# Sigmoid attention with a SiLU layer behind it: w_in's second half in two steps, and another order at the end

## Chip, cores and metric

The kernel runs on one core of one Trainium2 chip. The metric is the device time of one execution in microseconds (us); times of several runs are given by their median. TensorE is called PE, VectorE DVE, ScalarE ACT, GpSimd POOL and SyncE SP, as in the profile.

## What is computed

Eight batches of 448 tokens, with 12 heads of 64 each, go through attention with a sigmoid in place of the softmax; the result, 3584 tokens by 768, goes through a layer of 2048 hidden units with SiLU.

```python
scores = scale * np.matmul(q, k.transpose(0, 1, 3, 2)) - np.log(S)   # q, k, v: (8, 12, 448, 64)
attn = 1.0 / (1.0 + np.exp(-scores))
attn_out = np.matmul(attn, v)
x = attn_out.transpose(0, 2, 1, 3).reshape(B * S, H * D)             # (3584, 768)
h = x @ w_in                                                         # w_in: (768, 2048)
g = h * (1.0 / (1.0 + np.exp(-h)))
out = g @ w_out                                                      # w_out: (2048, 768)
```

All inputs and the output are float32 in DRAM. The kernel multiplies in float16.

## The kernel before

**Tiles.** The heads are taken four at a time, two pairs of them, as a *quad*; a batch has three quads, and there are 24 in all, numbered 0 to 23. A quad's k, q and v lie in the tiles kf, qf and vf, 224 KB each. k and q are transposed to kT and qT: for quads 0 to 5 by matmuls against an identity (pe_transpose, L143), for later ones by DMA transposes. The scores of a quad come in seven tiles (scores, L174), whose sigmoid ACT writes to attnT (L181); values (L205) multiplies them with v into xT, the transposed input of the layer.

**The layer.** For the first two batches, h_unit (L240) makes the hidden units in 16 chunks of 128 columns of w_in (fc 0 to 15), six matmuls each. Chunks 0 to 3 read w_in's first quarter of columns, 4 to 7 the second, 8 to 11 the third, 12 to 15 the fourth. From chunk 8 of the first batch on, w_in_sums also lets DVE form sums of w_in's halves (L280 to L284). Later batches are taken two at a time with a Strassen-Winograd scheme on such sums (h_pair, L316). The output product works in the same way: out_set takes two blocks of 128 tokens, a1 and a2, and seven products of eight matmuls (product, L463), each followed by one or two additions on DVE (plus, L473) that gather the four parts c11, c12 (tile osb[0], block one) and c21, c22 (osb[1], block two), each 128 x 384.

**Order.** The order on each engine is that of the program text. On PE the chunks of the layer are a generator that is advanced between the attention's bursts by their cost in ns; after the last burst the rest of it runs straight through. So the last call of out_set, with last=True, is the end of the kernel, and only DVE's additions and the stores stand behind its last product.

**Loads.** All loads but that of the first q are issued by POOL on one DMA queue, in program order, and cast to float16 on the way. load(names, g) issues one DMA per name. load_w_in(step, steps) issues two DMAs, each for half of w_in's rows: 384 KB each for a quarter of the columns, 768 KB each for half of them. after_transpose and after_values fix the order. It is, from w_in on: w_in quarter 0; k and q of quad 4; w_in quarter 1; k and q of quad 5; v of quad 3; w_in quarters 2 and 3 in one step; v of quad 4; w_out's parts 0 and 2; v of quad 5; k and q of quad 6; w_out part 1; k and q of quad 7; w_out part 3. The transposes of k and q of quads 4 and 5 stand between bursts 0, 1, 2 and 4 of the first stretch in which layer and attention are mixed.

**Stores.** store writes an osb tile to the output, 64 token rows with each of two DMAs, on the queues that it is given: whole rows (192 KB a DMA) or columns left or right (96 KB a DMA). In the last call the left half of block one is stored by SP alone after c11; block two is stored whole, one half of its rows by SP and the other by ACT, after c21; and c12 is made in two pieces of 192 columns, each with eight matmuls of its own, an addition, and a store of 48 KB by SP and one by ACT.

Of the kernel before, what the change touches and what calls it, by code (L numbers as in the profile page):

```python
# [17 lines left out]
def kernel(  # L18
# [9 lines left out]
    nc = tc.nc  # L28

    B, H, S, D = q.shape  # L30
    NT, DMODEL = out.shape
    DFF = moe_w_in.shape[1]
# [8 lines left out]
    NO2 = DMODEL // 2  # L41
    NQB = NQ * B
    NHC = NFC // 2
# [22 lines left out]
    def new_flat(name, g):  # L66
        flat[name, g] = (p3 if name == "v" else p4).tile(
            [P, 2, NCH, D], F16, tag=f"{name}f", name=f"{name}f"
        )

    def rows_in(name, g):
        b, iq = divmod(g, NQ)
        return (
            source[name][b]
            .rearrange("(j h) s d -> j h s d", j=2)[:, 2 * iq : 2 * iq + 2]
            .rearrange("j h (p c) d -> (h p) j (c d)", c=NCH)
        )

    def load(names, g, c0=0, c1=NCH):
        for name in names:  # L80
            if (name, g) not in flat:
                new_flat(name, g)
            nc.gpsimd.dma_start(  # L83
                flat[name, g][:, :, c0:c1].rearrange("p j c d -> p j (c d)"),
                rows_in(name, g)[:, :, c0 * D : c1 * D],
            )
# [13 lines left out]
    w_in_of = w_in_sb.rearrange("p (q h) f -> p h q f", h=2)  # L100
    w_out_sb = cpool.tile([P, NFC, DMODEL], F16, tag="w_out_sb", name="w_out_sb")

    def load_w_in(step, steps=1):
        cols = slice(step * DFF // 4, (step + steps) * DFF // 4)
        for j in range(2):
            rows = slice(j * DMODEL // 2, (j + 1) * DMODEL // 2)
            nc.gpsimd.dma_start(
                w_in_sb[j * D : (j + 1) * D, :, cols],
                moe_w_in[rows, cols].rearrange("(cc d) f -> d cc f", d=D),
            )  # L110

    def load_w_out(part):
        fcs = slice(part * NFC // 4, (part + 1) * NFC // 4)
        nc.gpsimd.dma_start(
            w_out_sb[:, fcs],
            moe_w_out[part * DFF // 4 : (part + 1) * DFF // 4].rearrange("(fc p) e -> p fc e", p=P),
        )
# [182 lines left out]
    def h_pair(m, tail):  # L300
# [112 lines left out]
    wq = [  # L413
        [w_out_sb[:, r * NHC : (r + 1) * NHC, c * NO2 : (c + 1) * NO2] for c in range(2)]
        for r in range(2)
    ]
    tw = {}
# [18 lines left out]
    def block(g):  # L436
        return gTr[:, :, g * P : (g + 1) * P]

    def row_blocks(m, g):
        return [rows_of[2 * m + u // NCH, u % NCH] for u in (2 * g, 2 * g + 1)]  # L440

    def out_set(a1, rows1, a2, rows2, scale, tail=(), last=False, halves=False):
        nonlocal hold
        lo, hi = slice(0, NHC), slice(NHC, NFC)
        osb = [p3.tile([P, DMODEL], F32, tag="osb", name="osb") for _ in range(2)]
        c11, c12 = (osb[0][:, nh * NO2 : (nh + 1) * NO2] for nh in range(2))
        c21, c22 = (osb[1][:, nh * NO2 : (nh + 1) * NO2] for nh in range(2))
        m1 = p3.tile([P, S], F32, tag="m1", name="m1")[:, :NO2]
        between, *sg = tail or [None]
        for i in range(len(sg) + 1, 4):  # L450
            sg.append(cpool.tile([P, NHC, P], F16, tag=f"S{i}", name=f"S{i}"))

        def store(rows, o, cols, engines):
            for at, (row, eng) in enumerate(zip(rows, engines)):
                eng.dma_start(row[:, cols], o[at * HP : (at + 1) * HP, cols])

        left, right, whole = slice(0, NO2), slice(NO2, DMODEL), slice(0, DMODEL)

        def product(a, w, between=None):
            po = ps_1.tile([P, 512], F32, tag="ps1", name="po")  # L460
            n = w.shape[2]
            for fc in range(NHC):
                nc.tensor.matmul(  # L463
                    po[:, :n], a[:, fc, :], w[:, fc, :], start=(fc == 0), stop=(fc == NHC - 1)
                )
                if fc < NHC - 1:
                    yield 163
                if between and fc == NHC // 2 - 1:
                    yield from between()
            return po[:, :n]  # L470

        def plus(o, po, x, sign=1.0):
            nc.vector.scalar_tensor_tensor(  # L473
                out=o, in0=po, scalar=sign * scale, in1=x, op0=ALU.mult, op1=ALU.add
            )

        if not tail:
            nc.vector.tensor_sub(sg[2], a1[:, lo], a2[:, lo])
            nc.vector.tensor_add(sg[0], a2[:, lo], a2[:, hi])
        po = yield from product(a1[:, lo], wq[0][0], between)  # L480
        nc.scalar.activation(m1, po, AF.Copy, scale=scale)
        sg.append(cpool.tile([P, NHC, P], F16, tag="S4", name="S4"))
        if not tail:
            nc.vector.tensor_sub(sg[1], sg[0], a1[:, lo])
        hold = False
        yield 163
        if tail:
            po = yield from product(sg[2], tw[3])
            plus(c22, po, m1)
            yield 163  # L490
        po = yield from product(a1[:, hi], wq[1][0])
        plus(c11, po, m1)
        nc.vector.tensor_sub(sg[3], a1[:, hi], sg[1])
        if last or halves:
            store(rows1, osb[0], left, (nc.sync, nc.sync))
        yield 163
        if not tail:
            po = yield from product(sg[2], tw[3])
            plus(c22, po, m1)
            yield 163  # L500
        po = yield from product(sg[1], tw[2])
        both = c21 if last else c22
        plus(both, po, c22)
        plus(c12, po, m1)
        yield 163

        def minus():
            po = yield from product(a2[:, hi], tw[4])
            plus(c21, po, both, -1.0)
            if not last:  # L510
                yield 163

        if not last:
            yield from minus()
        po = yield from product(sg[0], tw[1])
        plus(c22, po, both)
        plus(c12, po, c12)
        if last:
            yield 163
            yield from minus()  # L520
        store(rows2, osb[1], whole, (nc.sync, nc.scalar if last else nc.sync))
        yield 163
        for c0 in (0, NO2 // 2) if last else (0,):
            c1 = NO2 // 2 + c0 if last else NO2
            po = yield from product(sg[3], wq[1][1][:, :, c0:c1])
            plus(c12[:, c0:c1], po, c12[:, c0:c1])
            if last:
                store(rows1, osb[0], slice(NO2 + c0, NO2 + c1), (nc.sync, nc.scalar))
        if not last:
            store(rows1, osb[0], right if halves else whole, (nc.sync, nc.sync))  # L530
        yield 163

# [23 lines left out]
            if b * NFC + fc in rows_at:  # L556
                rows_of_quad(*rows_at[b * NFC + fc], act_copy)

    HALVES = 0

    def moe_set(m, g, tail=()):
        scale = ISX if m == 0 else 1.0
        step = out_set(
            block(g),
            row_blocks(m, g),
            block(g + 1),
            row_blocks(m, g + 1),
            scale,
            tail,
            halves=(m == B // 2 - 1 and g >= HALVES),  # L570
        )
        for i, ns in enumerate(step):
            if m % 2 == 0 and g == 2 and i % 8 == 4 and i < 32:
                fcs = slice(i // 8 * 4, i // 8 * 4 + 4)
                nc.vector.tensor_scalar_mul(kept[:, fcs], block(NCH - 1)[:, fcs], scale)
            if m == 0 and g == 2 and i in (36, 44, 52):
                next(in_sums)
            if m == 0 and g == 0 and i in (2, 8, 14, 20):
                next(sums)
            yield ns  # L580
# [59 lines left out]
    def after_transpose(g):  # L640
        if g == 0:
            load_w_in(0)
            load("kq", 4)
            load_w_in(1)
        elif g == 1:
            load("kq", 5)

    def after_values(g):
        if g == 0:
            load("v", 3)  # L650
            load_w_in(2, 2)
        elif g == 1:
            load("v", 4)
            load_w_out(0)
            load_w_out(2)
        elif g == 2:
            load("v", 5)
            load("kq", 6)
            load_w_out(1)
            load("kq", 7)  # L660
            load_w_out(3)
        elif 4 < g < NQB - 3:
            load("v", g + 3)
# [29 lines left out]
    def transposes(g, name):  # L693
        pe_transpose(g, ((name, 0, 4), (name, 4, NCH)))
        if name == "q":
            after_transpose(g)
# [82 lines left out]
    n = 2 * NT_B  # L779
    for m in range(1, B // 2):  # L780
        stop = min(2 * (m + 1) * NT_B + 4, len(units))
        bursts = bursts_to(n, stop)
        n = stop
# [51 lines left out]
```

## Time and profile before

| | us |
|---|---|
| median of 3 runs | 364.54 |
| the three runs | 363.94, 364.54, 367.28 |
| the profiled execution, its own time | 367.21 |
| its span, first to last instruction | 365.1 |
| busy in the span: ACT | 249.7 |
| busy in the span: DVE | 265.0 |

The profile is of one execution. Its times count from the start of its span. In a timeline row the columns are start, duration, engine, line, operation, tile written and tiles read with shapes, and the number of instructions merged in the row; the bracket gives the engine's idle time before and what ended it. In a windows row there follow, after the bounds, the busy time and count of PE, PE's weight loads, DVE, ACT and POOL, then the granted PE clock as a share of the full one, the share of the DMA engines and GB/s. In a DMA row the columns are what is written and read, the issuing queue, the operation, count, size of one and the time from issue to landing.

### The profile page before, as it was taken

Reading aid. Unit: us, or ns where it says so; the run is one execution under the profiler, and the core shown is the slowest. Engines: PE = TensorE matmul, PEld = TensorE weight load, DVE = VectorE, ACT = ScalarE, POOL = GpSimd, SP = SyncE. Lnnn points to the kernel's source line nnn. Section 1 sums busy time; section 2 is a strip of 40 time slices with the busy share of each in tenths; the row PEclk is TensorE's granted clock in tenths of the full one; section 3 lists DMA queues with packets and bytes.
Section 4 is the critical chain, followed back from the end, with each engine's and each line's share of the span. In section 5 each row is a group of like instructions: output and inputs, shape, how many; then the busy total and the mean of one; then the engine's idle time right before and its main releaser. Section 6 shows DMA issues by size and latency. Waiting matters only on the chain.

```text
span 365.1 us, 7677 instructions
## 1 busy us (share of the span) xinstructions
PE 355.9 (97%) x3029; PEld 182.9 (50%) x3029; DVE 265.0 (73%) x498; ACT 249.7 (68%) x363; POOL 61.8 (17%) x103
## 2 busy tenths in 40 slices
PE   8999799999999999999999999999999999999995
PEld 4544345444454555555445455555445455556663
DVE  3647479887879678787677667786777677778773
ACT  5998587697778767678777767758888766660000
POOL 8543210412505001100222201200100000000000
PEclk9999899999999999999999999999999999999999
DMA  8999999999899838405999752731965020003333
GB/s 136 196 205 210 208 206 170 135 195 139 139 202 175 147 95 114 59 0 96 172 165 216 148 113 50 105 49 24 154 95 133 19 69 0 3 0 87 88 87 85
DMA packets 63106, 42.78 MB, mean 117 GB/s; under 512 B 36064, under 2 KB 59232, under 8 KB 63072
## 3 DMA queue, kind: packets, MB, share of 16 engines
q0 software_dynamic: 24096, 22.58, 41.3%
q1 hardware_dynamic: 38592, 19.21, 26.9%
q10 hardware_dynamic: 384, 0.52, 0.4%
q8 instruction: 23, 0.38, 0.4%
q14 instruction: 11, 0.09, 0.1%
HBM read 45.61 MB, written 11.01 MB: 155 GB/s over the span
## 4 chain that ended last, share of the span: by engine, by line
PE 89%; DMA 9%; DVE 1%; issue 0%
PE po L463 36%; PE hy L316 11%; PE psc L174 10%; PE ph L240 8%; PE hz L316 7%; PE hx L316 7%; PE pav L205 7%; DMA w_in_sb<-in_moe_w_in_dram 5%; DMA kf<-in_k_dram 3%; DMA qs<-in_q_dram 1%; DVE qT L150 1%; PE ptrq L143 0%; PE pw L130 0%; PE ptrk L143 0%; DVE qf L633 0%
## 5 line engine op out<-in xcount | busy, mean ns | idle before, releaser
L181 ACT ACTIVATE attnT<-psc 128x896 f16<-128x896 f32 x168 | 144.9, 922 | 32.5 <-PE psc L174 29.9
L463 PEld LDWEIGHTS <-S 128*128 128x128 f16 x456 | 42.2, 98 | 35.5 <-issue 10.4
L174 PE MATMUL psc<-qT,kT 64*64 64x448 f16 x672 | 52.2, 361 | 1.0 <-DVE qT L150 0.7
L473 DVE SCALAR_TENSOR_TENSOR osb<-po,osb 128x384 f32<-128x384 f32 (+1 forms) x71 | 37.8, 549 | 15.9 <-PE po L463 15.0
L221 DVE TENSOR_SCALAR xT<-pav 128x448 f16<-128x448 f32 x44 | 25.6, 620 | 26.0 <-PE pav L205 26.0
L327 ACT ACTIVATE gTr<-u 128x448 f16<-128x448 f32 x48 | 27.6, 575 | 23.2 <-DVE u L340 19.1
L240 PE MATMUL ph<-xT,w_in_sb 128*128 128x448 f16 x192 | 40.5, 361 | 2.7 <-DMA w_in_sb<-in_moe_w_in_dram 2.6
L463 PE MATMUL po<-w_out_sb,S 128*128 128x384 f16 (+1 forms) x232 | 41.5, 321 | 0.0
L463 PE MATMUL po<-T,S 128*128 128x384 f16 x224 | 41.3, 327 | 0.0
L316 PEld LDWEIGHTS <-w_in_sb 128*128 128x128 f16 x288 | 28.2, 98 | 26.1
L463 PEld LDWEIGHTS <-gTr 128*128 128x128 f16 x304 | 28.3, 98 | 23.2 <-issue 5.8
L205 PE MATMUL pav<-attnT,vf 64*64 64x448 f16 x672 | 37.5, 349 | 0.0
L463 PE MATMUL po<-w_out_sb,gTr 128*128 128x384 f16 x192 | 35.7, 327 | 0.0
L316 PE MATMUL hy<-xs,w_in_sb 128*128 128x448 f16 x144 | 35.1, 353 | 0.0
L316 PE MATMUL hx<-xT,w_in_sb 128*128 128x448 f16 x144 | 34.6, 353 | 0.0
L316 PEld LDWEIGHTS <-W 128*128 128x128 f16 x216 | 21.1, 98 | 19.6
L174 PEld LDWEIGHTS <-kT 64*64 64x64 f16 x672 | 16.2, 104 | 28.8 <-issue 24.2
L83 POOL DMA_DIRECT2D vf<-in_v_dram x24 | 17.2, 718 | 71.6 <-PE psc L174 70.0
L240 PEld LDWEIGHTS <-w_in_sb 128*128 128x128 f16 x192 | 17.7, 99 | 23.0 <-issue 8.9
L473 DVE SCALAR_TENSOR_TENSOR osb<-po,m 128x384 f32<-128x384 f32 x42 | 23.0, 553 | 6.4 <-PE psc L174 1.7
L253 DVE TENSOR_TENSOR gTr<-ph,tsig 128x448 f16<-128x448 f32 x32 | 19.8, 623 | 9.1 <-ACT tsig L252 8.9
L205 PEld LDWEIGHTS <-vf 64*64 64x64 f16 x672 | 20.1, 107 | 11.5 <-issue 1.1
(76 smaller groups left out, 414.4 us busy)
## 6 DMA issues: line engine op xcount, KB each, us to landing
out_dram<-osb SPq DMA_DIRECT2D x47, 192.0 KB, 3.2
vf<-in_v_dram POOLq DMA_DIRECT2D x24, 224.0 KB, 7.8
kf<-in_k_dram POOLq DMA_DIRECT2D x23, 224.0 KB, 5.8
qf<-in_q_dram POOLq DMA_DIRECT2D x23, 224.0 KB, 6.8
w_out_sb<-in_moe_w_out_dram POOLq DMA_DIRECT2D x4, 768.0 KB, 18.4
w_in_sb<-in_moe_w_in_dram POOLq DMA_DIRECT2D x4, 384.0 KB, 11.4
w_in_sb<-in_moe_w_in_dram POOLq DMA_DIRECT2D x2, 768.0 KB, 15.1
out_dram<-osb SPq DMA_DIRECT2D x14, 96.0 KB, 2.2
```

What stands on the lines that cost most here:

```text
L83: nc.gpsimd.dma_start(flat[name, g][:, :, c0:c1].rearrange("p j c d -> p j (c d)"), rows_in(name, g)[:, :, c0 * D : c1 * D],)
L150: (copy[0] if copy else nc.vector.tensor_copy)(dst[:, c0 * P : c1 * P], ptr[:, : (c1 - c0) * P])
L174: nc.tensor.matmul(psc[own, j, :S], qkT["k", g][rows, ch, own], qkT["q", g][rows, :, own], start=True, stop=True,)
L181: nc.scalar.activation(attnT[g, ch], psc[:, :, :S], AF.Sigmoid, bias=NEG_LOG_S, scale=QKSCALE)
L205: nc.tensor.matmul(pav[half][j * D : (j + 1) * D, :S], flat["v", g][own, j, ch, :], at[own, j, :], start=(ch == 0), stop=(ch == NCH - 1),)
L221: nc.vector.tensor_scalar_mul(xT[b][:, half * NQ + iq, :], pav[half][:, :S], SX)
L240: nc.tensor.matmul(ph[:, :S], w_in_of[:, cc // NQ, cc % NQ, fc * P : (fc + 1) * P], xT[b][:, cc, :], start=(at == 0), stop=(at == NCC - 1),)
L253: nc.vector.tensor_mul(gTr[:, fc, (b % 2) * S : (b % 2) * S + S], ph[:, :S], tsig)
L316: nc.tensor.matmul(ps, a[:, c, i * P : (i + 1) * P], bs(c), start=(first and c == 0), stop=(c == HCC - 1), skip_group_check=True,)
L327: nc.scalar.activation(gTr[:, side * NHC + i, odd * S : (odd + 1) * S], src, AF.Silu, scale=ISX)
L463: nc.tensor.matmul(po[:, :n], a[:, fc, :], w[:, fc, :], start=(fc == 0), stop=(fc == NHC - 1))
L473: nc.vector.scalar_tensor_tensor(out=o, in0=po, scalar=sign * scale, in1=x, op0=ALU.mult, op1=ALU.add)
```

## The change

Three things are changed.

w_in's second half is loaded in two steps of a quarter each, so by four DMAs of 384 KB instead of two of 768 KB. The place in the queue is the same.

q of quad 4 is issued behind w_in's second quarter instead of ahead of it.

In the last call of out_set, the product that is subtracted (a2[hi] with tw[4], for c21) moves from behind the product of sg[0] with tw[1] to ahead of it, as in all other calls. Block two is stored in two halves of its columns, the left behind c21 and the right behind c22, each with one DMA of 96 KB on SP and one on ACT. The last product, of sg[3] with wq[1][1], is made with eight matmuls of 384 columns, one addition, and one store of 96 KB on each of the two queues. The variable HALVES, which was 0 and so changed nothing, goes.

```diff
-    def load_w_in(step, steps=1):
-        cols = slice(step * DFF // 4, (step + steps) * DFF // 4)
+    def load_w_in(step):
+        cols = slice(step * DFF // 4, (step + 1) * DFF // 4)
...
         po = yield from product(sg[1], tw[2])
-        both = c21 if last else c22
-        plus(both, po, c22)
+        plus(c22, po, c22)
         plus(c12, po, m1)
         yield 163
-
-        def minus():
-            po = yield from product(a2[:, hi], tw[4])
-            plus(c21, po, both, -1.0)
-            if not last:
-                yield 163
-
-        if not last:
-            yield from minus()
+        po = yield from product(a2[:, hi], tw[4])
+        plus(c21, po, c22, -1.0)
+        if last:
+            store(rows2, osb[1], left, (nc.sync, nc.scalar))
+        yield 163
         po = yield from product(sg[0], tw[1])
-        plus(c22, po, both)
+        plus(c22, po, c22)
         plus(c12, po, c12)
         if last:
-            yield 163
-            yield from minus()
-        store(rows2, osb[1], whole, (nc.sync, nc.scalar if last else nc.sync))
+            store(rows2, osb[1], right, (nc.sync, nc.scalar))
+        else:
+            store(rows2, osb[1], whole, (nc.sync, nc.sync))
         yield 163
-        for c0 in (0, NO2 // 2) if last else (0,):
-            c1 = NO2 // 2 + c0 if last else NO2
-            po = yield from product(sg[3], wq[1][1][:, :, c0:c1])
-            plus(c12[:, c0:c1], po, c12[:, c0:c1])
-            if last:
-                store(rows1, osb[0], slice(NO2 + c0, NO2 + c1), (nc.sync, nc.scalar))
-        if not last:
+        po = yield from product(sg[3], wq[1][1])
+        plus(c12, po, c12)
+        if last:
+            store(rows1, osb[0], right, (nc.sync, nc.scalar))
+        else:
             store(rows1, osb[0], right if halves else whole, (nc.sync, nc.sync))
         yield 163
...
         if g == 0:
             load_w_in(0)
-            load("kq", 4)
+            load("k", 4)
             load_w_in(1)
+            load("q", 4)
...
             load("v", 3)
-            load_w_in(2, 2)
+            load_w_in(2)
+            load_w_in(3)
```

More of the change, by code (lines that the diff above doesn't have):

```diff
@@ L460, in product @@
             po = ps_1.tile([P, 512], F32, tag="ps1", name="po")
-            n = w.shape[2]
             for fc in range(NHC):
                 nc.tensor.matmul(
-                    po[:, :n], a[:, fc, :], w[:, fc, :], start=(fc == 0), stop=(fc == NHC - 1)
+                    po[:, :NO2], a[:, fc, :], w[:, fc, :], start=(fc == 0), stop=(fc == NHC - 1)
                 )
@@ L469, in product @@
                     yield from between()
-            return po[:, :n]
+            return po[:, :NO2]
         def plus(o, po, x, sign=1.0):
@@ L557, in moe_h @@
                 rows_of_quad(*rows_at[b * NFC + fc], act_copy)
-    HALVES = 0
     def moe_set(m, g, tail=()):
@@ L569, in moe_set @@
             tail,
-            halves=(m == B // 2 - 1 and g >= HALVES),
+            halves=(m == B // 2 - 1),
         )
```

## Prediction

> **What bounds the kernel now.** I read the page first: busy time, the granted clock by slices, the chain of waits.
>
> ```profile
> span 365.1 us, 7677 instructions
> PE 355.9 (97%) x3029; PEld 182.9 (50%) x3029; DVE 265.0 (73%) x498; ACT 249.7 (68%) x363; POOL 61.8 (17%) x103
> ...
> PEclk9999899999999999999999999999999999999999
> ...
> PE 89%; DMA 9%; DVE 1%; issue 0%
> ```
>
> TensorE (PE) is busy for 97% of the span and carries 89% of the chain, so time is won only where PE stands still or runs slowly, or behind its last product. The one dent in the granted clock is the fifth slice, 36.5 to 45.6 us. The chain in order of time and the waits of PE name the place.
>
> ```profile
> 24.83 16.55 DMA w_in_sb<-in_moe_w_in_dram
> 41.52 0.92 PE ph L240 x4
> ...
> 324.87 35.78 PE po L463 x228
> ```
>
> ```profile
> PE ph L240 <- DMA w_in_sb<-in_moe_w_in_dram: 2.6, 1, 2.6
> ```
>
> The chain hangs on a w_in load issued at 24.83 and landing 16.55 later, at 41.38; from 41.52 it is nearly all PE. The timeline of PE there, and the windows that hold the clock (column after the five engines), show the price.
>
> ```profile
> 31.03 0.58 PE L143 MATMUL ptrq<-ident,qf 128*64 128x128 f16 x14
> 34.36 1.88 PE L240 MATMUL ph<-xT,w_in_sb 128*128 128x448 f16 x9
> 38.19 0.74 PE L240 MATMUL ph<-xT,w_in_sb 128*128 128x448 f16 x3
> 41.52 0.92 PE L240 MATMUL ph<-xT,w_in_sb 128*128 128x448 f16 x4 [2.59 <-DMA w_in_sb<-in_moe_w_in_dram]
> 42.87 0.96 PE L143 MATMUL ptrq<-ident,qf 128*64 128x128 f16 x14
> 43.76 3.07 PE L240 MATMUL ph<-xT,w_in_sb 128*128 128x448 f16 x9
> ```
>
> ```profile
> 43.00:43.50 0.50, 0.50 (x12) 0.50 (x13) 0.00 (x0) 0.50 (x1) 0.06 (x1) 0.50 1.17 212
> 46.50:47.00 0.50, 0.50 (x10) 0.14 (x8) 0.03 (x1) 0.32 (x1) 0.05 (x1) 1.00 1.24 208
> ```
>
> PE stands still for 2.59 us before the first product on w_in's second half (chunk fc 8). Then the clock is at 0.50: the 14 transposes take 0.96 instead of 0.58, the 9 products 3.07 instead of 1.88. Stall and slow clock cost 2.59 + 0.38 + 1.19 = 4.16 us.
>
> The Trainium skill, "TensorE: Matmul & The Clock Gate", Part 1, says that the clock is judged over a free-running window of 3413 ns and halved after an idle one, and its closing table warns of gaps over about 3 us. The trace agrees on the half clock, but shows it behind a gap of only 2.59 us. By the free phase the same gap would be punished in some executions and not in others.
>
> **Part 1, w_in's second half in two steps.** The timeline of GpSimd (POOL) has the issues of v of quad three, of the later of the two big loads, of w_in's second quarter (two) and of v of quad five; the DMA view behind it gives the time from issue to landing (last column) of these five in the same order.
>
> ```profile
> 21.74 0.70 POOL L83 DMA_DIRECT2D vf<-in_v_dram  x1 [0.80 <-PE psc L174]
> 24.83 0.66 POOL L107 DMA_DIRECT2D w_in_sb<-in_moe_w_in_dram  x1 [0.85 <-DMA kf<-in_k_dram]
> 16.09 0.66 POOL L107 DMA_DIRECT2D w_in_sb<-in_moe_w_in_dram  x1 [1.16 <-DMA vf<-in_v_dram]
> 17.22 0.66 POOL L107 DMA_DIRECT2D w_in_sb<-in_moe_w_in_dram  x1 [0.47 <-DMA kf<-in_k_dram]
> 30.75 0.70 POOL L83 DMA_DIRECT2D vf<-in_v_dram  x1 [0.40 <-issue]
> ```
>
> ```profile
> vf<-in_v_dram POOLq DMA_DIRECT2D x1, 224.0 KB, 11.4
> w_in_sb<-in_moe_w_in_dram POOLq DMA_DIRECT2D x1, 768.0 KB, 16.5
> w_in_sb<-in_moe_w_in_dram POOLq DMA_DIRECT2D x1, 384.0 KB, 11.5
> w_in_sb<-in_moe_w_in_dram POOLq DMA_DIRECT2D x1, 384.0 KB, 12.1
> vf<-in_v_dram POOLq DMA_DIRECT2D x1, 224.0 KB, 19.7
> ```
>
> v of quad three lands at 21.74 + 11.4 = 33.14 and the last big load at 41.38, so the 2 x 768 KB take 8.24 us. Cut into four loads of 384 KB at the same rate, 2.06 each, w_in's third quarter is there at 33.14 + 4.12 = 37.26. The small loads of the second quarter land at 27.59 and 29.32, 1.73 apart; by that it is 36.6. PE wants it at 38.19 + 0.74 = 38.93. I take 37.26: the stall goes with 1.67 us to spare, and the slow clock with it, since no gap is left in front of it.
>
> The fourth quarter still lands at about 41.4. Its first product is the 25th from 41.52 on:
>
> ```profile
> 51.09 1.31 PE L240 MATMUL ph<-xT,w_in_sb 128*128 128x448 f16 x6
> 55.63 1.52 PE L205 MATMUL pav<-attnT,vf 64*64 64x448 f16 x28
> ```
>
> It falls in the first of these rows, at 51.09 - 4.16 = 46.9 or later, 5.5 us behind its load. The four 0.66-us issues lie on POOL, busy for 17%. The bytes ahead of every later load are unchanged, so later landings stay where they are while their readers come up to 4.16 us earlier. The nearest is v of quad five: it lands at 30.75 + 19.7 = 50.45, read from 55.63 - 4.16 = 51.47. That is 1.0 us of cover.
>
> **Part 2, quad four's q behind the second quarter.** It moves back past two loads of 384 KB and lands where the second of them did, at 29.32. Its transposes start at 31.03: 1.7 us of cover, cost nothing. Each microsecond beyond that would be one of PE. The second quarter gains one q load of time, which PE does not need.
>
> **Part 3, the end.** The rows are of the timeline, then of the DMA view. The product order changes (the subtracted product before the c22 one), with the same matmuls; the 16 narrow matmuls become 8 wide ones.
>
> ```profile
> 357.86 1.46 PE L463 MATMUL po<-T,gTr 128*128 128x384 f16 x8
> 359.16 1.48 PE L463 MATMUL po<-w_out_sb,S 128*128 128x192 f16 x16
> 357.24 0.55 DVE L473 SCALAR_TENSOR_TENSOR osb<-po,m 128x384 f32<-128x384 f32 x1
> 360.68 0.36 DVE L473 SCALAR_TENSOR_TENSOR osb<-po,osb 128x192 f32<-128x192 f32 x1 [0.30 <-PE po L463]
> 361.15 0.83 SPq L455 DMA_DIRECT2D out_dram<-osb  x1
> 361.50 0.72 ACTq L455 DMA_DIRECT2D out_dram<-osb  x1
> ```
>
> ```profile
> out_dram<-osb ACTq DMA_DIRECT2D x1, 48.0 KB, 2.6
> out_dram<-osb SPq DMA_DIRECT2D x14, 96.0 KB, 2.2
> out_dram<-osb ACTq DMA_DIRECT2D x1, 192.0 KB, 3.4
> ```
>
> Eight wide matmuls take 1.46 where 16 narrow ones take 1.48: PE ends 0.02 earlier. The last addition is 0.55 instead of 0.36: 0.19 later, from 360.66 to 361.21. SP issues 0.11 after it now (361.04 to 361.15), but ACT only at 361.50, behind its own earlier stores. With the block before stored in halves, its left half leaves once the subtracted product is added, near 358.7, so both queues should be free and issue at 361.32. The last landing is now 361.50 + 2.6 = 364.1. For the new 96 KB stores the bounds are 2.2 (a store alone) and 3.4 (192 KB beside another queue); I take 2.6, nearest to a last store with both queues in use: 363.92. The end gains 0.2, bounds +0.6 and -0.6.
>
> **The sum** on the profiled execution, 367.21 (span 365.1 and 2.1 around it), is 367.21 - 4.16 - 0.2 = 362.85. Of the three runs, two lie at 363.94 and 364.54 and one at 367.28, as long as the profiled one. So the median, 364.54, lacks 2.67 us that the profile shows. If all of it sits in stall and clock, the changed median is 362.85; if only the 1.57 us of slow clock does, it is 364.54 - 2.59 - 0.2 = 361.75. Nothing shown parts these two, and I take the middle: **362.3 us**, on its own 361.4 to 363.5 with the end's bounds.
>
> **The rivals.**
> First, the median run carries the whole 4.16 and the 2.67 comes from elsewhere: 364.54 - 4.16 - 0.2 = 360.2. For it: stall and clock are the only large losses that PE shows. Against it: a difference of 3 us between runs fits a gap that is punished in some and not in others.
>
> Second, the loads don't do what they say: the third quarter still lands after 38.93 because four loads on one queue share its rate and finish together, or the median has no stall at all. Then only the end is left: 364.3. Against it: landings in the trace come in order of issue, 1.73 us apart for the small ones.
>
> Third, slower: every load has a fixed cost, and two more of them push the whole queue back. Price: a 96 KB store takes 2.2 us alone, nearly all of it fixed. Two more loads would then put v of quad five at 50.45 + 4.4 = 54.85, read at 51.47: PE stands still for 3.4 us in a new place and pays the slow clock again, 362.3 + 3.4 + 1.57 = 367.3. It decides from 1.0 us of delay on, and makes the kernel slower than its median from about 1.7. Against it: 2 x 384 KB need 3.5 us in the queue by the 1.73 above, less than the 4.12 of one 768 KB load, so the fixed part seems to lie beside other transfers.
>
> The Trainium skill speaks for this rival: "DMA: Bandwidth & Descriptors", Rules for kernel authors, asks for 1 MiB or more per DMA, and its section on the anatomy of one DMA fits about 2.0 us plus the bytes. By that 2.0 the third rival would give an estimated 366.9; the 1.73 us between landings goes against adding it per load.
>
> **How the numbers follow.** Forecast 0.50, first rival 0.24, second 0.13, third 0.13. The range takes in the first two rivals with the end's bounds: 359.8 (360.2 less 0.4) to 365.0 (364.3 and up to 0.7); the third stays out. A measurement of this kernel can tell about 1% from no change, 3.6 us. Below 360.9: the first rival and 0.03 of the forecast, 0.27. Above 368.2: the worse part of the third rival, 0.05. Between: 0.68.
>
> **What would show it.** Part 1: the first product on the second half waits for nothing, w_in's third quarter lands near 37.3, the clock has no 0.50 rows near 43, and PE's wait for w_in is gone from the list. Part 2: no wait of the transposes at 31 for q. Part 3: last addition 0.55, last stores issued together near 0.1 behind it. Wrong would be a new wait of PE for v of quad five or for q, PE idle of more than 0.5 us between 36 and 52, or a changed median under 360.9 or over 363.5.

## The result and the profile after

| | before | changed |
|---|---|---|
| median of 21 runs, us | 364.31 | 363.35 |
| lowest and highest, us | 363.05, 370.08 | 361.94, 364.60 |
| ratio of the times, 95% interval | | 0.9965 [0.9949, 0.9981] |
| profiled execution, its span, us | 367.21, 365.1 | 361.94, 360.1 |

The change is worth 0.35% by the ratio (0.2 to 0.5%), which is 1.3 us, and 1.0 us by the medians. The two profiled executions differ by 5.3 us, so they are not typical ones; the first is one of the long executions of the kernel before, the second the shortest of the changed kernel. Six of the 21 executions of the kernel before took more than 366 us, and two of 80 in the later sets; why they are long was not followed up. What an ordinary one looks like came out of further profiles, below.

The page of the changed kernel first: span, PE's busy time, the granted clock and the chain.

```profile
span 360.1 us, 7663 instructions
PE 354.0 (98%) x3021; PEld 181.7 (50%) x3021; DVE 264.6 (73%) x497; ACT 249.6 (69%) x363; POOL 63.0 (17%) x105
...
PEclk9999999999999999999999999999999999999999
...
PE 94%; ACT 3%; DMA 1%; DVE 1%; issue 0%
```

The dent in the clock is gone, and no w_in load is left in the chain. The timeline of PE at w_in's second half, and all the waits of PE in this execution:

```profile
38.05 1.50 PE L240 MATMUL ph<-xT,w_in_sb 128*128 128x448 f16 x7
39.48 0.57 PE L174 MATMUL psc<-qT,kT 64*64 64x448 f16 x8
```

```profile
PE pw L130 <- DVE warm L620: 1.1, 1, 1.1
PE psc L174 <- DVE qT L150: 0.7, 2, 0.4
```

The last three matmuls of chunk 7 and the first four of chunk 8 run as one row of seven: nothing separates them. The issues of the last load of w_in's third quarter and of the last of its fourth, and behind them their times to landing:

```profile
23.69 0.66 POOL L107 DMA_DIRECT2D w_in_sb<-in_moe_w_in_dram  x1 [0.50 <-DMA kf<-in_k_dram]
27.70 0.66 POOL L107 DMA_DIRECT2D w_in_sb<-in_moe_w_in_dram  x1 [1.46 <-DMA w_in_sb<-in_moe_w_in_dram]
```

```profile
w_in_sb<-in_moe_w_in_dram POOLq DMA_DIRECT2D x1, 384.0 KB, 11.9
w_in_sb<-in_moe_w_in_dram POOLq DMA_DIRECT2D x1, 384.0 KB, 11.7
```

They land at 35.6 and 39.4. The end, in the timeline and the DMA view:

```profile
354.70 1.46 PE L462 MATMUL po<-w_out_sb,S 128*128 128x384 f16 x8
356.20 0.56 DVE L472 SCALAR_TENSOR_TENSOR osb<-po,osb 128x384 f32<-128x384 f32 x1 [0.28 <-PE po L462]
356.79 0.47 SPq L455 DMA_DIRECT2D out_dram<-osb  x1
356.79 0.50 ACTq L455 DMA_DIRECT2D out_dram<-osb  x1
```

```profile
out_dram<-osb SPq DMA_DIRECT2D x1, 96.0 KB, 2.1
out_dram<-osb ACTq DMA_DIRECT2D x1, 96.0 KB, 2.4
```

Both last stores go out at once, 0.03 us behind the addition. From the start of the last product to the end of the span it is 360.1 - 354.70 = 5.40 us, where it was 365.1 - 359.16 = 5.94. This stretch hardly depends on what came before it: in the six profiles with the old end it is 5.93 to 6.02, in the six with the changed end 5.39 to 5.48. So one profile gives it to about 0.1.

### The profile page after: what moved, and what is told of

Its sections match the earlier page's. It is cut to its first block, busy times and chain, and to the rows that moved or that the text cites. A ratio compares the mean times of both kernels' runs of the same rounds, so it can differ in the third digit from the quotient of the medians.

```text
span 360.1 us, 7663 instructions
## 1 busy us (share of the span) xinstructions
PE 354.0 (98%) x3021; PEld 181.7 (50%) x3021; DVE 264.6 (73%) x497; ACT 249.6 (69%) x363; POOL 63.0 (17%) x105
## 4 chain that ended last, share of the span: by engine, by line
PE 94%; ACT 3%; DMA 1%; DVE 1%; issue 0%
PE po L462 37%; PE hy L316 11%; PE psc L174 11%; PE ph L240 11%; PE pav L205 8%; PE hz L316 8%; PE hx L316 8%; ACT attnT L181 3%; DMA qs<-in_q_dram 1%; PE ptrk L143 1%; PE ptrq L143 1%; DVE qT L150 1%; PE pw L130 0%; DVE qf L623 0%; DVE osb L472 0%
## 5 line engine op out<-in xcount | busy, mean ns | idle before, releaser
L472 DVE SCALAR_TENSOR_TENSOR osb<-po,osb 128x384 f32<-128x384 f32 x70 | 37.6, 554 | 15.8 <-PE po L462 15.0
L462 PE MATMUL po<-w_out_sb,S 128*128 128x384 f16 x224 | 41.3, 327 | 0.0
L240 PE MATMUL ph<-xT,w_in_sb 128*128 128x448 f16 x192 | 39.2, 353 | 0.0
L383 DVE TENSOR_TENSOR u<-hy,p 128x448 f32<-128x448 f32 x24 | 15.0, 625 | 13.8 <-PE hy L316 13.4
```

Of the source, the lines that this page charges most:

```text
L240: nc.tensor.matmul(ph[:, :S], w_in_of[:, cc // NQ, cc % NQ, fc * P : (fc + 1) * P], xT[b][:, cc, :], start=(at == 0), stop=(at == NCC - 1),)
L383: nc.vector.tensor_add(u3, y, p1)
L462: nc.tensor.matmul(po[:, :NO2], a[:, fc, :], w[:, fc, :], start=(fc == 0), stop=(fc == NHC - 1))
L472: nc.vector.scalar_tensor_tensor(out=o, in0=po, scalar=sign * scale, in1=x, op0=ALU.mult, op1=ALU.add)
```

## The experiments

The ratio is to the kernel before, timed beside it on the same chip; it is not the quotient of two medians. The kernels were timed in three sets: the first four of the table (the kernel before at 364.34 there), the next three (364.32), and the last two, on another chip (364.03). Medians are compared within a set.

| kernel | median, us | ratio, 95% interval |
|---|---|---|
| new loads alone (e1_loads) | 364.16 | 0.9985 [0.9963, 1.0006] |
| new end alone (e2_end) | 363.10 | 0.9968 [0.9950, 0.9986] |
| q of quad four later, alone (e3_q4) | 364.04 | 0.9999 [0.9980, 1.0018] |
| gap filled (e4_filled) | 365.76 | 1.0035 [1.0009, 1.0061] |
| changed kernel again (after_again) | 363.16 | 0.9966 [0.9938, 0.9994] |
| changed, quad eight's k, q early (e5_kq8) | 363.41 | 0.9979 [0.9963, 0.9996] |
| before, quad eight's k, q early (e6_before_kq8) | 364.43 | 0.9998 [0.9978, 1.0019] |
| changed, another order of loads (e7_order) | 362.37 | 0.9952 [0.9937, 0.9967] |
| changed, q of quad four back (e10_q_back) | 362.77 | 0.9962 [0.9946, 0.9978] |

**The parts, one at a time.** The theory was that the loads make most of the gain.

```diff
-            load_w_in(2, 2)
+            load_w_in(2)
+            load_w_in(3)
```

> The kernel before with one part of the change: w_in's second half in two steps. Theory (the loads make the gain): the first product on the second half waits for nothing, no half clock near 43 us, and the median is 0.6 to 1.2 us below the kernel before (ratio near 0.997), since ordinary executions carry only about 1 us of the gap. Rival (the whole 4.16 us sits in ordinary executions): ratio near 0.989. Rival (the end makes the gain): no wait in the trace either, but the median equal to the kernel before within 0.3 us.

Measured: 0.9985, an interval that holds no change; the gain is 0.5 us by the ratio and 0.2 by the medians. The wait for w_in's second half was gone, as expected, but the gain lay below the least expected, and by the medians it is where the last rival had it. The twelve runs fall into two groups, five from 362.35 to 363.05 and seven from 363.97 to 365.48; the profiled one, 364.38, belongs to the second. In its profile the lost time had moved: DVE waits for q of quad eight, and PE waits at the first output product for the hidden units (gTr) that DVE is late with. Both rows are of the timeline:

```profile
74.42 0.62 DVE L158 COPY qr<-qf 128x896 f16<-128x896 f16 x1 [2.86 <-DMA qf<-in_q_dram]
76.69 1.46 PE L463 MATMUL po<-w_out_sb,gTr 128*128 128x384 f16 x8 [1.17 <-DVE gTr L253]
```

For the end alone, the kernel before got the changed out_set, with its loads as they were.

> The kernel before with the new end alone: loads as before. Theory: PE still waits for w_in near 39 us (0 to 2.6 us); from the start of the last addition to the end of the span 3.9 us instead of 4.4; the median 0.2 to 0.5 us lower. Rival (the end makes the whole gain): the median 1.0 us lower or more.

Measured: 0.9968, 1.2 us by the medians, where the rival had it, though the interval reaches from 0.5 to 1.8. By the ratios the end alone brings as much as the whole change (0.9965). Its stretch from the last product (355.20) to the end of the span (360.6) is 5.40, as in the changed kernel. The end is therefore worth 0.54 by the trace, a little above what the theory had; what the rest of the 1.2 is, no trace shows. In this execution there was next to no gap at w_in, with the big loads:

```profile
38.36 1.67 PE L240 MATMUL ph<-xT,w_in_sb 128*128 128x448 f16 x7
```

Seven products in 1.67 instead of 1.50: at most 0.17 us of waiting. The same loads that cost 2.59 in the first profile cost next to nothing here: the second of them landed at 38.95 and not at 41.38.

```diff
-            load("kq", 4)
+            load("k", 4)
             load_w_in(1)
+            load("q", 4)
```

> The kernel before with one part of the change: quad four's q issued behind w_in's second quarter. Theory: q lands 3.5 us later, near 29.3, still ahead of its transposes at 31, so nothing waits for it, and the median stays within 0.3 us of the kernel before. Rival (the cover of 1.7 us is gone in ordinary executions): a wait of the transposes for q, and a median 0.5 us or more above.

Measured: 0.9999, and no transpose waits for q. Neither a cost nor a gain shows. The reverse, the changed kernel with q back in its old place, was run too:

> The changed kernel with quad four's q issued ahead of w_in's second quarter again. Theory: q lands 3.5 us earlier and nobody uses it; no new wait, and the median within 0.3 us of the changed kernel (363.3). Rival (the second quarter becomes late, with less than 1 us of cover): PE waits for w_in near 29 us and the median is 0.5 us above.

Measured: 362.77 and 0.9962, against 0.9965 for the changed kernel; the intervals overlap almost wholly. PE waited for no w_in load. Part 2 is neutral by both runs, as far as these intervals tell.

**How large the gap is in ordinary executions.** Ten matmuls that nobody reads fill the place where PE stood still.

```diff
+        if b == 0 and fc == NHC:
+            keep_busy(10)
```

> The kernel before with ten idle matmuls of 512 columns (0.213 us each, 2.1 us) ahead of the first product on w_in's second half; their output is read by nobody. They lie in the gap where there is one. If the half clock comes from the gap, it is gone, and an execution with the full gap of 2.59 us takes 1.57 us less. For the median: an ordinary gap of about 1.1 us gives 1.0 us above the kernel before; a full gap of 2.6 us without the half clock gives no change; no gap in ordinary executions gives 2.1 us above.

Measured: 1.0035, 1.4 us by the medians, against 2.1 us of added work. So the ordinary gap hides some 0.7 us of it; by the interval, 0.3 to 2.2 us of cost, it can be anything from none to 1.8. Windows behind it show the full clock:

```profile
43.00:44.00 1.00, 1.00 (x21) 0.70 (x18) 0.57 (x1) 1.00 (x2) 0.00 (x0) 1.00 1.15 209
```

Whether the filling keeps the clock up this doesn't tell, since the next profile has the full clock without it. The kernel before was profiled a second time.

> The kernel before, unchanged, for a second profile. Theory: the profile of 367.21 us was of a long execution; an ordinary one has a gap of 0.5 to 1.5 us ahead of the first product on w_in's second half and the clock stays at 1.00 behind it; the span is near 362.5. Rival (the gap is always near 2.6 us, and the ordinary runs are faster elsewhere): 2.6 us again.

Measured: 364.31 us, exactly the median. The timeline of PE:

```profile
38.35 0.74 PE L240 MATMUL ph<-xT,w_in_sb 128*128 128x448 f16 x3
40.46 0.92 PE L240 MATMUL ph<-xT,w_in_sb 128*128 128x448 f16 x4 [1.36 <-DMA w_in_sb<-in_moe_w_in_dram]
...
68.49 1.88 PE L240 MATMUL ph<-xT,w_in_sb 128*128 128x448 f16 x9
...
76.61 1.46 PE L463 MATMUL po<-w_out_sb,gTr 128*128 128x384 f16 x8
```

```profile
42.00:44.00 2.00, 2.00 (x23) 1.02 (x18) 1.22 (x3) 1.90 (x3) 0.19 (x1) 1.00 1.16 209
```

The gap is 1.36 us, and the window behind it, of the view by windows, has the clock at 1.00. In the profile of e3_q4, with the same big loads, the gap is 1.43, also at the full clock. (The view puts that one down to DVE, whose gTr ended at 40.46. But the load landed at 40.41, and in e2_end the same product did not wait for this gTr.) In e6_before_kq8, below, it is 0.23. The gap follows the landing of the second big load: 38.95, 39.33, 40.29, 40.41 and 41.33 by the DMA view, with gaps of 0.17, 0.23, 1.36, 1.43 and 2.59. That is the spread of one pair of loads.

**Where the rest went.** The changed kernel, profiled and timed again:

> The changed kernel, unchanged. Theory: no gap ahead of w_in's second half; DVE waits 1 to 3 us for q of quad eight near 72 us, because POOL gives out that load only when the transposed q of quad six is there, near 64.5; where that wait passes 2 us, PE waits for gTr near 75. Median 0.7 to 1.9 us below the kernel before.

Measured: 363.16 and 0.9966; the profiled execution took 362.65. The same places in PE's timeline, and DVE's longest wait for a DMA there:

```profile
66.82 1.88 PE L240 MATMUL ph<-xT,w_in_sb 128*128 128x448 f16 x9
...
75.50 1.46 PE L462 MATMUL po<-w_out_sb,gTr 128*128 128x384 f16 x8 [0.44 <-DVE gTr L253]
```

```profile
DVE qr L158 <- DMA qf<-in_q_dram: 2.0, 1, 2.0
```

At 68.49 against 66.82 the changed kernel leads by 1.67 us, a little more than the gap. At the first output product, 76.61 against 75.50, it leads by 1.11. So 0.56 us is given back in between, where PE waits for gTr. The expectation had put that wait behind a wait of DVE of over 2 us; it came at 2.0. Over the profiles PE's wait grows with DVE's wait for k and q of quad eight: 0.44 at 1.97, 0.61 at 2.2 (e10_q_back), 0.68 at 2.35 (e9_whole), 1.17 at 2.86 (e1_loads), and none at 1.57, which is the second profile of the kernel before, or below. So about 1.6 us of DVE's wait cost PE nothing.

Why q of quad eight does not come earlier, although everything ahead of it does: POOL gives that load out only once the transposed q of quad six is there (the small copy to seen), and starting that transpose earlier does not bring it much earlier. Rows of the timeline and the DMA view, the kernel before first:

```profile
61.35 1.22 SPq L159 DMA_TRANSPOSE qT<-qr  x1
65.52 0.18 POOL L671 COPY seen<-qT 1x1 f16<-1x1 f16 x1 [14.96 <-DMA qT<-qr]
```

```profile
qT<-qr SPq DMA_TRANSPOSE x1, 4.1
```

and the changed kernel, first profile:

```profile
56.89 3.06 SPq L159 DMA_TRANSPOSE qT<-qr  x1
64.53 0.60 POOL L663 COPY seen<-qT 1x1 f16<-1x1 f16 x1 [15.30 <-DMA qT<-qr]
```

```profile
qT<-qr SPq DMA_TRANSPOSE x1, 7.6
```

The transpose is issued 4.46 us earlier and is done 1.0 us earlier; it takes 7.6 us instead of 4.1. The rows of the kernel before are of its long execution, so here are the same rows of the two second profiles, the kernel before first again:

```profile
58.71 1.98 SPq L159 DMA_TRANSPOSE qT<-qr  x1
65.19 0.18 POOL L671 COPY seen<-qT 1x1 f16<-1x1 f16 x1 [15.19 <-DMA qT<-qr]
```

```profile
57.05 3.53 SPq L159 DMA_TRANSPOSE qT<-qr  x1
65.19 0.18 POOL L663 COPY seen<-qT 1x1 f16<-1x1 f16 x1 [15.41 <-DMA qT<-qr]
```

Issued 1.66 us earlier, it is there at the same time. What goes with its landing is the last load given out ahead of it: in seven profiles, in which that load lands anywhere from 61.7 to 67.5, the transposed q of quad six lands 0.7 to 1.8 us behind it. The time to landing also holds the transpose of k, which was issued 2.27 us before on the same queue and lands 0.8 to 0.9 us ahead.

A first remedy was to load k and q of quad eight ahead of that condition.

```diff
             load("v", g + 3)
+            if g == 5:
+                load("kq", 8)
...
-                load("kq", 8)
```

> The changed kernel, with k and q of quad eight loaded behind v of quad eight, near 49 us, instead of behind the transposed q of quad six. Theory (the gain of the loads is given back at quad eight's q): q lands before 68, DVE no longer waits for it, PE does not wait for gTr, and the median is 0.3 to 1.2 us below the changed kernel. Rival (the ordinary changed runs lose their time elsewhere): no change.

> The kernel before, with k and q of quad eight loaded as early as in e5_kq8. Theory: here the gap at w_in's second half makes DVE late by itself, so that q of quad eight is seldom waited for; the median stays within 0.5 us of the kernel before, and the step from here to e5_kq8 is larger than the one from the kernel before to the changed one: 1.5 to 2.2 us.

The first missed: 363.41, no better than the changed kernel beside it (363.16). The second stayed at the kernel before, 364.43, as expected, but the step from it to e5_kq8 is 1.0 us and not 1.5 to 2.2. DVE did stop waiting for q of quad eight, but the wait moved to PE. From e5_kq8, the waits, the timeline and the time of the transpose issued at 57.42:

```profile
PE psc L174 <- DMA qT<-qr: 1.6, 1, 1.6
```

```profile
68.33 0.21 POOL L665 COPY seen<-qT 1x1 f16<-1x1 f16 x1 [15.91 <-DMA qT<-qr]
```

```profile
qT<-qr SPq DMA_TRANSPOSE x1, 10.8
```

With two more loads in the crowded stretch the transpose takes 10.8 us to landing, and now the scores of quad six wait for it. The profile of e6_before_kq8 is of an execution of 367.21 us, as long as the first profile's. Its gap at w_in is 0.23 and its clock behind that stays up; PE waits 1.2 us for a transposed q at 100 us and again at 117. So the gap is not what every long execution has in common.

This fits a theory in which the DMA engines are the bound in that stretch, so that a load moved into it only pushes a transpose back. By windows of the changed kernel their busy share, which passes 1 in this view, is 1.23 from 50 to 64 us and 0.79 from 66 to 68. If the theory is right, a load has to be taken out.

```diff
-        elif 4 < g < NQB - 3:
+        elif 5 < g < NQB - 3:
...
+                load("kq", 8)
                 load("v", 6)
-                load("kq", 8)
                 load("v", 7)
+                load("v", 8)
```

> The changed kernel with two loads put in another order: v of quad eight leaves its place near 49 us and comes last behind the transposed q of quad six (k and q of quad eight, then v of six, seven and eight). No load is moved into the crowded stretch, one of 224 KB is taken out of it. Theory (the DMA engines are the bound from 50 to 70 us, so that transposes and loads only push each other): the transposed q of quad six is there about 1 us earlier, q of quad eight about 2 us earlier, DVE no longer waits for it (2.0 us in the second look at the changed kernel), PE waits neither for gTr nor for qT, and the median is 0.3 to 0.7 us below the changed kernel (363.3), ratio near 0.995. Rival (v of six or seven becomes late, or the time is lost elsewhere): 363.3 or above.

Measured: 362.37, in six runs from 362.06 to 362.52, ratio 0.9952. The profile, POOL, PE and DVE:

```profile
63.29 0.18 POOL L663 COPY seen<-qT 1x1 f16<-1x1 f16 x1 [18.03 <-DMA qT<-qr]
```

```profile
66.58 1.88 PE L240 MATMUL ph<-xT,w_in_sb 128*128 128x448 f16 x9
...
74.66 1.46 PE L462 MATMUL po<-w_out_sb,gTr 128*128 128x384 f16 x8
```

```profile
70.25 0.61 DVE L158 COPY kr<-kf 128x896 f16<-128x896 f16 x1
70.77 0.61 DVE L158 COPY qr<-qf 128x896 f16<-128x896 f16 x1
```

The last load ahead now lands at 61.7 (63.1 and 63.9 in the two profiles of the changed kernel), the transposed q of quad six is there at 63.29 (64.53 and 65.19), the two copies of quad eight follow each other without a wait, and PE waits for neither gTr nor qT. Against the second profile of the kernel before, the lead at the first output product is 76.61 - 74.66 = 1.95 us, and it was 68.49 - 66.58 = 1.91 before that point: nothing is given back. The nearest kernel of the same set is e10_q_back, the changed kernel but for the neutral part 2: 362.77, so this version is 0.4 us faster by the medians, in the range of the theory. The intervals of the two overlap (0.9937 to 0.9967 against 0.9946 to 0.9978), so the 0.4 us is not settled by the times, while the absent wait is seen in the trace.

**The two halves of the new end.** One kernel divides the last product again and keeps the stored halves of block two; the other keeps the undivided product and stores block two whole.

```diff
...
-        po = yield from product(sg[3], wq[1][1])
-        plus(c12, po, c12)
+        for c0 in (0, NO2 // 2) if last else (0,):
+            c1 = NO2 // 2 + c0 if last else NO2
+            po = yield from product(sg[3], wq[1][1][:, :, c0:c1])
+            plus(c12[:, c0:c1], po, c12[:, c0:c1])
...
```

> The changed kernel with the last product in two pieces of 192 columns again, each with its own addition and stores; block two stays stored in halves. Read in the trace from the start of the last eight matmuls' worth of product to the end of the span: 5.94 us in the kernel before, 5.40 in the changed one. Theory (the gain comes from stores that no longer stand behind one another on ACT): between, near 5.6. Rival (the halves of block two alone make the gain): 5.2, since the last addition is 0.19 us shorter and the last store smaller.

```diff
-        if last:
-            store(rows2, osb[1], left, (nc.sync, nc.scalar))
...
-            store(rows2, osb[1], right, (nc.sync, nc.scalar))
+            store(rows2, osb[1], whole, (nc.sync, nc.scalar))
```

> The changed kernel with block two stored whole, by one DMA on each queue behind the c22 addition; the last product undivided. From the start of the last product to the end of the span: theory (whole rows just ahead keep the DMA engines busy and hold the last store up): 5.6 to 6.0 us. Rival (the undivided last product alone makes the gain): 5.4.

From the start of the last product to the end of the span: 360.8 - 354.93 = 5.87 with the divided product, 361.5 - 355.47 = 6.03 with the whole block; 5.94 in the kernel before, 5.40 in the changed one. Neither part alone brings more than 0.1 in its one profile; the rival of e8_divided (5.2) is out, and so is that of e9_whole (5.4). The 5.87 is also farther up than the 5.6 that e8_divided's theory had; e9_whole lies at the upper end of its theory's 5.6 to 6.0. From e9_whole, the last stores in the DMA view:

```profile
out_dram<-osb SPq DMA_DIRECT2D x1, 96.0 KB, 2.7
out_dram<-osb ACTq DMA_DIRECT2D x1, 96.0 KB, 2.8
```

Behind 192 KB on each queue the same last stores take 2.7 and 2.8 us instead of 2.1 and 2.4. That covers most of what e9_whole loses. In e8_divided the last store of ACT goes out at 357.24, 0.36 us behind its addition, since ACT was still at the one before. But it lands at 359.4, 4.5 us from the start of the last product, and in the changed kernel that is 4.5 too. What the divided end loses lies wholly behind the last landing, 1.4 us instead of 0.9, and why was not followed up.

## Why the prediction was right, and where it was not

The time lay in the range and the direction was right, but the gain is 1.0 us by the medians and not 2.2, and it came from other parts than forecast. That the time fell in the range owes much to the range's width, 359.8 to 365.0, which holds even the unchanged 364.54. The end, sized at 0.2, gives 0.5 to 0.6 by the traces. The loads made up nearly all of the forecast 2.2; what is left for them is 0.4 us by the medians and 0.7 by the ratio. That is a difference and not a measurement: alone they are not told from no change, and the end alone brings as much as the whole.

The profiles can be split at the first output product. From there to the end of the span it is 285.9 to 286.0 us in five of the six with the old end (288.8 in e6_before_kq8) and 285.3 to 285.4 in the six with the changed end. That is the end's part, in every pair. Up to there it is 75.22 to 76.62 us with the old loads where the clock stayed up and nothing was filled in, 79.20 in the long first profile, 74.74 to 75.51 in the changed kernel and its kin (e8, e9, e10), and 76.69 with the new loads alone. These groups touch, so the size of the loads' part in an ordinary execution stays open.

**Part 1, landing times.** Right in kind, off in size. The third quarter landed at 35.6 where 37.26 was taken and 36.6 stood as the other bound; the fourth at 39.4 and not 41.4. The wait of PE is in none of the eight profiles with the four loads, and neither is a half clock there. The landing, however, moves from run to run by more than the step that was argued over, as the next point shows.

**Part 1, the price.** This is the step that failed. It was sized by a middle between two cases: all of the missing 2.67 us in stall and clock, or only the clock's 1.57 of it. The profile of 367.21 us was of a long execution. The gap is 1.36 in an execution of the median's length and 0.17 to 1.43 in three others with the old loads, without the half clock, where the sum used 4.16 - 2.67 = 1.49 in the first case and 2.59 in the second. The first was the nearer one. The upper bounds were also added up 0.1 short: 362.85 and 364.34 with 0.8 for the end are 363.65 and 365.1; it changes nothing here.

**Part 1, what is late next.** "The nearest is v of quad five" was wrong: v of quad five was waited for in none of the changed profiles. The next one was q of quad eight. The step looked only for loads whose landing time stays where it is, and overlooked a load that is given out on a condition: behind a transpose that lands after the loads ahead of it, however early it starts. PE waits for what follows from it for 0 and 0.44 us in the two profiles of the changed kernel, and for 1.17 in that of the new loads alone; of the lead over the second profile of the kernel before, 0.56 is given back.

**Part 2** held: no cost and no gain that the runs show.

**Part 3** had the right mechanism and too small a size: 0.54 against 0.2, within its bound of 0.6. The last store took 2.4 instead of 2.6, both queues issued 0.03 instead of 0.11 behind the addition, and the rest of the span behind the last landing was 0.9 instead of 1.0. That neither edit alone brings much was not foreseen.

**The rivals.** The first, with the whole 4.16 in the median, falls by the second profile. The second was right in that the end brings a good part of the gain alone, at more than the 0.2 it had for it; that the third quarter lands late was wrong. The third, a fixed cost per load, falls: the last of the four loads landed at 39.4 to 40.6, the second of the two at 38.95 to 41.33, and v of quad five was never late. The Trainium skill's rule of larger DMAs ("DMA: Bandwidth & Descriptors", Rules for kernel authors) did not decide here. In the changed kernel's first profile the 384 KB loads landed 1.9 to 2.0 us apart; the 768 KB loads landed 3.7 to 4.4 apart, so no cost of the division shows.

## What to carry to other kernels

When the profiled execution is longer than the median, take the largest stall of the profile as an upper end, and profile the same kernel again before pricing it; here it was 2.59, 1.36 and 0.17 us in the same place. A long execution need not be long for the reason that its profile shows first. When a stall goes, look not only at loads that land at a fixed time but at those given out on a condition that itself runs on the crowded resource. Where the DMA engines are busy throughout, try taking out what is needed later: here two loads moved into such a stretch brought a transposed tile at 68.3 instead of 64.5 to 65.2, and one load taken out brought it at 63.3.

## What was not expected of the hardware

A gap of 2.59 us on PE, in one execution, was followed by some 3.4 us at half clock, from 42.8 to 46.2 and so from 1.3 us behind the gap's end, and gaps of 1.36 and 1.43 by none. A DMA transpose of one quad took 4.1, 7.6 or 10.8 us from issue to landing; the landing goes with that of the last load ahead, and not with the issue. From 20 us on POOL gave each load out 0.25 to 0.6 us behind the landing of the eighth one before it, 16 times in a row in the first profile of the changed kernel; whether the queue or the program sets that is not shown. One load of the unchanged program landed at 41.38 in one execution and 40.3 in another; why was not found.
